# A DCN-v2 cross network on one core: filler matmuls as column tiles instead of full-array matmuls

## The chip, the cores and the metric

The kernel runs on one core of a Trainium2 chip. The metric is device time in microseconds (us), the median of several executions. The core has TensorE (PE) for matmuls, VectorE (DVE), ScalarE (ACT) and GpSimd (POOL) for the rest, and SyncE (SP), which here only issues DMAs. PEld in the profile is TensorE's weight load, which can run beside its matmuls.

## The reference

The input `x0` has 4096 rows of 416 features in bf16. There are six layers, each with a 416x416 matrix `ws[l]` and a bias `bs[l]`. The recurrence is

```
x = x0
for l in range(6):
    x = x0 * (x @ ws[l] + bs[l]) + x
return x
```

## The kernel before, in words

The kernel holds the activations transposed: features on the 128 partitions, rows of the batch along the free axis. The 416 features are three chunks of 128 and a tail of 32. The batch is cut into four slabs of 1024 rows, and each slab runs through six layers: 24 layer steps in all. A step takes the two halves (512 rows) of its slab through the 3x3 chunk products and adds the products with the tail. VectorE adds the bias and multiplies by `x0` on the way out of PSUM (line 445). ScalarE and GpSimd treat the tail (lines 474, 497 and 188). The `+ x` of the recurrence stays in PSUM: the matmuls of all layers of a slab accumulate there, and only the first one of a slab sets `start`.

Every engine has its own instruction list, written out by hand, and semaphores between them. Nothing is scheduled by a planner.

TensorE's array is addressed in tiles. The helper `tile_mm` (line 201 issues the matmul) uses 128 rows and 32 columns of the array, the q-th of four column tiles, and writes to the 32 PSUM partitions of that tile. The main matmuls are such groups of four: same moving operand, four different slices of 32 weight columns. The tail's products (lines 341 and 356) use 32 rows and 128 columns.

TensorE's list begins as follows.

1. `fill(14)` (line 233): 14 matmuls with constant operands of 1.0 (line 210). Their result in PSUM bank 7 is never read. They wait for no semaphore of the kernel.
2. A wait for the identity matrix, made by GpSimd, and for two loads of the input, each 256 rows, issued by SP and ACT as their first instructions (lines 113 and 460).
3. Twelve transposes of 128x128 (line 239), full-array, into PSUM. VectorE (line 420) and ScalarE (line 467) copy them to `x0T_sb`.
4. The first layer step of the first slab: for the first feature chunk three groups of column tiles, likewise for the second, then `third_input` (the transposes of 256 more rows, as column tiles), `tail_inputs`, `bias_sums`, and the third chunk. The weights of the first layer come in two loads, issued by SP (line 114) and ACT (line 461).

After this the steps follow each other on TensorE. At the end of the last slab the output is transposed back on TensorE, partly as column tiles (`out_chunk`), partly as full-array transposes (line 394), and stored.

The line numbers in the profile of before are those of this kernel.

## Time and profile before

| What | Value |
|---|---|
| Median of 5 runs | 131.71 us (131.37 to 131.87) |
| The profiled execution's own time | 131.87 us |
| Its span in the profile | 130.0 us |
| Time of that execution outside the span | 1.87 us |
| TensorE busy | 124.2 us (96%), 2406 matmuls |
| VectorE, ScalarE, GpSimd busy | 100.3, 71.4, 22.7 us |
| Mean granted TensorE clock | 0.992 |

The span runs from the first to the last instruction of the program on the core. A row of the profile names the line, the engine, the operation, the output and the inputs; `x14` is a count, and a mean or a minimum, median and maximum of durations in ns follow. "128*128 128x256" means an array tile of 128 rows by 128 columns, and an operand of 128 partitions with 256 elements. The ends of matmuls are modelled by the profiler, and matmuls overlap in the pipeline: how fast the array works is read from the distance between the starts, not from the duration of one. In the slices of the page each digit is a fortieth of the span.

### The profile page before, as it was taken

The page shows a single profiled execution, that of the slowest core. Times are in us where ns is not written, and L with a number is a line of the kernel's source. Part 1 is how long each engine was busy: PE and PEld are TensorE (multiplying, and loading weights), DVE is VectorE, ACT ScalarE, POOL GpSimd, SP SyncE. Part 2 cuts the span into 40 slices and gives each one's busy share as a digit, 9 for nine tenths or more (in the row PEclk, how much of TensorE's full clock was granted, in tenths as well). Part 3 has the DMA queues.
Part 4 walks back from the last instruction along what each step waited for, and adds up shares of the span by engine and source line. Part 5 has one row for each costly group of instructions (what it writes and reads, how often), then busy time and mean ns, then how long its engine had stood idle before and what let it go on. Part 6 is the DMA issues. An engine that isn't in the chain of part 4 may idle for free.

```text
span 130.0 us, 5323 instructions
## 1 busy us (share of the span) xinstructions
PE 124.2 (96%) x2406; PEld 62.4 (48%) x2406; DVE 100.3 (77%) x154; ACT 71.4 (55%) x164; POOL 22.7 (17%) x41
## 2 busy tenths in 40 slices
PE   7999999999999999999999999999999999999950
PEld 5654444444444444444444544444444444444530
DVE  2359779779779779779779779779779779779760
ACT  0537357377737357377737357377737357357650
POOL 7602202202202202202202212202202202202400
PEclk9999999999999999999999999999999999999996
DMA  4999989991009561000009434000009661000036
GB/s 127 284 281 298 215 117 228 155 194 40 8 12 145 113 212 55 5 0 5 0 17 172 83 120 147 0 5 0 5 14 131 122 225 42 5 0 5 3 84 183
DMA packets 32934, 12.54 MB, mean 96 GB/s; under 512 B 25338, under 2 KB 32912, under 8 KB 32912
## 3 DMA queue, kind: packets, MB, share of 16 engines
q1 hardware_dynamic: 31536, 11.49, 42.5%
q10 hardware_dynamic: 1184, 0.67, 1.8%
q8 instruction: 19, 0.31, 1.0%
q0 software_dynamic: 192, 0.05, 0.2%
q14 instruction: 3, 0.02, 0.1%
HBM read 2.90 MB, written 3.41 MB: 48 GB/s over the span
## 4 chain that ended last, share of the span: by engine, by line
PE 95%; DVE 1%; issue 0%; DVEq 0%
PE ps L201 81%; PE ps L341 10%; PE ps L210 2%; PE ps L239 1%; DVE o_sb L450 1%; PE ps L394 0%; DVE x0T_sb L425 0%; DVEq L33 0%; PE ps L356 0%
## 5 line engine op out<-in xcount | busy, mean ns | idle before, releaser
L445 DVE SCALAR_TENSOR_TENSOR xT_sb<-ps,cb_sb,x0T_sb 128x512 bf16<-128x512 f32 x120 | 80.8, 743 | 17.0 <-PE ps L341 17.0
L201 PE MATMUL ps<-xT_sb,w_sb 128*32 128x512 bf16 (+1 forms) x1680 | 89.0, 364 | 0.0
L201 PEld LDWEIGHTS ps<-xT_sb,w_sb 128*32 128x32 bf16 x1680 | 43.0, 97 | 38.7 <-issue 4.2
L474 ACT ACTIVATE xt_sb<-xt_sb 32x256 bf16<-32x256 bf16 x80 | 33.1, 414 | 16.6 <-POOL xt_sb L188 15.9
L497 ACT ACTIVATE t_sb<-ps,cb_sb 64x256 f32<-64x256 f32 x48 | 22.5, 468 | 30.7 <-PE ps L201 30.4
L188 POOL TENSOR_TENSOR xt_sb<-t_sb,x0t_sb 128x256 bf16<-128x256 f32 x20 | 13.4, 671 | 83.1 <-ACT t_sb L497 83.1
L201 PE MATMUL ps<-x0T_sb,w_sb 128*32 128x512 bf16 (+1 forms) x336 | 18.5, 365 | 0.0
L445 DVE SCALAR_TENSOR_TENSOR xo_sb<-ps,cb_sb,x0T_sb 128x512 bf16<-128x512 f32 x23 | 15.6, 744 | 3.4 <-PE ps L341 3.3
L341 PE MATMUL ps<-xt_sb,wt_sb 32*128 32x512 bf16 x80 | 12.3, 380 | 0.0
L201 PEld LDWEIGHTS ps<-x0T_sb,w_sb 128*32 128x32 bf16 x336 | 8.4, 97 | 7.6 <-issue 1.0
L510 ACT ACTIVATE x0t_sb<-x_sb 32x256 bf16<-32x256 bf16 x24 | 9.9, 413 | 0.4
L356 PE MATMUL ps<-xt_sb,wt_sb 32*128 32x512 bf16 x40 | 7.8, 385 | 0.0
L341 PE MATMUL ps<-xt_sb,wc_sb 32*128 32x256 bf16 x80 | 7.7, 268 | 0.0
L341 PEld LDWEIGHTS ps<-xt_sb,wt_sb 32*128 32x128 bf16 x80 | 2.4, 92 | 8.5 <-DVE xT_sb L445 8.5
L341 PEld LDWEIGHTS ps<-xt_sb,wc_sb 32*128 32x128 bf16 x80 | 3.9, 93 | 2.4 <-issue 0.2
L188 POOL TENSOR_TENSOR xot_sb<-t_sb,x0t_sb 128x256 bf16<-128x256 f32 x4 | 2.7, 672 | 12.6 <-ACT t_sb L497 12.6
L210 PE MATMUL ps<-const-bfloat16-1.0 128*128 128x256 bf16 x14 | 3.1, 415 | 0.8 <-PEq L547 0.8
L467 ACT ACT_TABLE_LOAD x1 | 1.3, 1283 | 3.4 <-issue 3.4
L420 DVE COPY x0T_sb<-ps 128x256 bf16<-128x256 bf16 x4 | 1.0, 290 | 2.7 <-PE ps L239 2.7
L210 PEld LDWEIGHTS ps<-const-bfloat16-1.0 128*128 128x128 bf16 x14 | 1.9, 141 | 1.6 <-issue 0.8
L341 PE MATMUL ps<-x0t_sb,wt_sb 32*128 32x512 bf16 x16 | 2.4, 380 | 0.0
L173 POOL DMA_DIRECT2D wc_sb<-in_ws_dram x4 | 2.2, 554 | 0.0
(45 smaller groups left out, 29.0 us busy)
## 6 DMA issues: line engine op xcount, KB each, us to landing
out_dram<-o_sb SPq DMA_DIRECT2D x3, 832.0 KB, 4.2
w_sb<-in_ws_dram SPq DMA_DIRECT2D x5, 312.0 KB, 4.1
xin_sb<-in_x_dram SPq DMA_DIRECT2D x2, 208.0 KB, 3.3
out_dram<-o_sb SPq DMA_DIRECT2D x1, 256.0 KB, 3.7
xin_sb<-in_x_dram ACTq DMA_DIRECT2D x1, 208.0 KB, 3.0
w_sb<-in_ws_dram ACTq DMA_DIRECT2D x1, 208.0 KB, 3.7
out_dram<-o_sb ACTq DMA_DIRECT2D x1, 208.0 KB, 3.2
out_dram<-o_sb SPq DMA_DIRECT2D x1, 208.0 KB, 3.2
```

The costliest lines, as they stand in the source:

```text
L173: pool.dma_start(wc_sb[lane(g), a:b, 32 * g:32 * g + 32], ws[a:b, DF:D, DF:D].rearrange("l p n -> p l n")).then_inc(s_wc[i], 16)
L188: pool.tensor_tensor(out=dst, in0=t32_sb[:, n % 2, :], in1=x0t_sb[:, s, 0:G], op=ALU.mult).then_inc(s_xt, 1)
L201: return pe.matmul(dst, lhsT=lhsT, rhs=rhs, start=start, stop=True, skip_group_check=True, tile_position=(0, 32 * q),)
L210: pe.matmul(ps[:, 7, 0:256], lhsT=const[:, 0:128], rhs=const, start=True, stop=True)
L239: ins = pe.transpose(out=psT[:, IN_BANKS[h][c], (j % 2) * 128:(j % 2 + 1) * 128], in_=xin_sb[:, j, c * 128:(c + 1) * 128], identity=ident[ ...
L341: return pe.matmul(dst, lhsT=lhsT, rhs=srct[lane(g), cols], start=l == 0 and start, stop=True, skip_group_check=True, tile_position=(32 * ...
L356: pe.matmul(ps[:, NC * h + 2, :], lhsT=wt_sb[lane(g), l, 0:128], rhs=srct[lane(g), :].rearrange("p (b r) -> p b r", b=2)[:, ::-1, :], star ...
L445: dve.scalar_tensor_tensor(out=dst, in0=ps[:, NC * half + c, :], scalar=cb_sb[:, c, l:l + 1], in1=x0T_sb[:, c, o:o + H], op0=ALU.add, op1= ...
L450: dve.tensor_copy(out=o_sb[:, j0 + 4:j0 + 8, 0:256], in_=psT[:, 4, :].rearrange("p (j d) -> p j d", d=256)).then_inc(s_oeD, 1)
L474: ins = act.activation(out=buf[lane(g), G:2 * G], in_=buf[lane(g ^ 1), 0:G], func=ACTF.Copy)
L497: ins = act.activation(out=t32_sb[HALVES[h], n % 2, :], in_=tail(h), func=ACTF.Identity, bias=cb_sb[HALVES[h], NC, l:l + 1],)
L510: ins = act.activation(out=x0t_sb[lane(g), s + 1, swap * G:(swap + 1) * G], in_=x4_sb[96:128, s, r * G:(r + 1) * G], func=ACTF.Copy,)
```

## The change

The filler's inner matmul is split. One matmul with a weight operand of 128x128 and a moving operand of 128x256 becomes four with 128x32 weights, one in each column tile, each with the same moving operand. The four write the same 128 partitions by 256 columns of bank 7 as the one did. The count of filler steps, 14, stays, as does their place in the list. The operands are the same constants.

```
             def fill(n):
                 for i in range(n):
-                    pe.matmul(ps[:, 7, 0:256], lhsT=const[:, 0:128], rhs=const, start=True, stop=True)
+                    for q in range(4):
+                        tile_mm(ps[lane(q), 7, 0:256], const[:, 0:32], const, q, True)
```

The helper it calls is the one of the main matmuls:

```
            def tile_mm(dst, lhsT, rhs, q, start):
                return pe.matmul(
                    dst, lhsT=lhsT, rhs=rhs, start=start, stop=True,
                    skip_group_check=True, tile_position=(0, 32 * q),
                )
```

TensorE's list then has 56 filler matmuls and 56 weight loads in place of 14 and 14. All lines after the filler move down by one, so that line 239 of before is line 240 after. The matmuls of the filler appear under line 201, the helper's, after the change.

## The prediction

> **What bounds the kernel now.** I read the page first: busy shares, the row of the granted clock, the chain that ended last. Then the start, where the change lies: the chain from 0 to 9 us, TensorE in order of time, and the durations by line.

> ```profile
> PE 124.2 (96%) x2406; PEld 62.4 (48%) x2406; DVE 100.3 (77%) x154; ACT 71.4 (55%) x164; POOL 22.7 (17%) x41
> ...
> PEclk9999999999999999999999999999999999999996
> ...
> PE 95%; DVE 1%; issue 0%; DVEq 0%
> PE ps L201 81%; PE ps L341 10%; PE ps L210 2%; PE ps L239 1%; DVE o_sb L450 1%; PE ps L394 0%; DVE x0T_sb L425 0%; DVEq L33 0%; PE ps L356 0%
> ```

> TensorE is busy for 96% of the span and makes up 95% of the chain. What delays its start is not made up later: the 24 layer steps run back to back on it. So the question is how the first 5 us change.

> ```profile
> 0.80 0.04 issue
> 0.85 3.14 PE ps L210 x14
> 3.99 1.27 PE ps L239 x12
> 5.26 1.55 PE ps L201 x32
> 6.81 0.03 issue
> 6.83 0.43 DVE x0T_sb L425
> ```

> The chain starts with the filler (L210) and goes on through the input transposes (L239) and the first layer (L201). The filler is thus on the path. Next, durations of one instruction (minimum, median, maximum):

> ```profile
> L210 PEld LDWEIGHTS ps<-const-bfloat16-1.0 x14: 105/147/147, 0.8 to 3.4; 128*128 128x128 bf16 x14
> L210 PE MATMUL ps<-const-bfloat16-1.0 x14: 371/418/418, 0.8 to 3.6; 128*128 128x256 bf16 x14
> ...
> L239 PE MATMUL ps<-ident,xin_sb x12: 298/311/312, 3.8 to 5.0; 128*128 128x128 bf16 x12
> ...
> L394 PE MATMUL ps<-ident,xo_sb x12: 219/219/229, 124.2 to 125.0; 128*128 128x128 bf16 x12
> ```

> The same transpose takes 311 ns at 3.8 to 5.0 us and 219 ns at the end. The row of the granted clock shows 9 in the first slices too, but these durations say that the array ran slower there. The spacing says by how much: twelve transposes start from 3.79 to 5.26 - 0.298 = 4.96, so (4.96 - 3.79) / 11 = 0.106 us apart. A transpose of four column tiles in the first layer is 0.056 us after the one before (28 instructions, seven groups of four, in 0.56 us, less 0.22 for the last). The filler: (0.85 + 3.14 - 0.418 - 0.85) / 13 = 0.21 us apart. So the array runs at half speed up to about 5.1 us, and at full speed from the first layer on:

> ```profile
> 0.85 3.14 PE L210 MATMUL ps<-const-bfloat16-1.0 128*128 128x256 bf16 x14 [0.85 <-PEq L547]
> 3.79 1.47 PE L239 MATMUL ps<-ident,xin_sb 128*128 128x128 bf16 x12
> 5.19 1.48 PE L201 MATMUL ps<-x0T_sb,w_sb 128*32 128x512 bf16 x24
> 6.49 0.56 PE L201 MATMUL ps<-ident,xin_sb 128*32 128x128 bf16 x27
> ```

> 24 matmuls of 512 columns are six groups of four; six groups in 1.48 us, with 0.38 for the last, are 0.22 us apart. At half speed they would be 0.43 apart. The full clock comes about 4.3 us after the first filler matmul (0.85 to 5.1).

> ```profile
> xin_sb<-in_x_dram SPq DMA_DIRECT2D x1, 208.0 KB, 2.8
> xin_sb<-in_x_dram ACTq DMA_DIRECT2D x1, 208.0 KB, 3.0
> ```

> Both input loads are issued at 0.81 and land at 3.6 and 3.8. The last filler matmul starts at 3.57 and streams until 3.57 + 0.21 = 3.79, when the first transpose starts. Filler and data end together here, with 0.2 us between them at most.

> **The change part by part.**

> Removed: 14 matmuls of 128x256 with 128-column weights, 0.21 us apart. Added: 56 matmuls of 32x256, in 14 groups of four column tiles. If the four run side by side, a group takes the time of one full matmul. The trace shows this at full speed: a group of 128 columns every 0.056 us, and the full-array L394 of 128 columns also every 0.056 ((124.64 - 124.24) / 7). No row shows column tiles at half speed. Bounds for a group: 0.21 us (all side by side) and 4 x 0.21 = 0.85 (one after the other). I take 0.21, because every group of four in this trace runs side by side; the term is 0.

> Weight loads: 14 of 147 ns become 56 of about 97 ns (the 128x32 rows of L201). In the first layer four such loads fit even in a group's 0.056 us, so in 0.21 us they are hidden. What hides them is the streaming of the group before; with that cover gone they would cost up to 56 x 0.097 = 5.4 us. [...]

> The filler's order, its waits (none) and its PSUM bank (7) stay. The transposes still wait for the same loads. No other engine's instructions, no DMA and no queue is moved. TensorE gets 84 more instructions, of 64 bytes (0.31 MB of instruction traffic over 4812 of them): 5 KB more to fetch. No fetch stall shows before; I cost it at 0, up to 0.1.

> The one new step: the array changes from column tiles to full tiles ahead of the first transpose. Before, filler and transposes had the same shape. Such a change shows a gap in the trace, from the end of streaming to the next start:

> ```profile
> 124.02 0.28 PE L201 MATMUL ps<-ident,xot_sb 128*32 128x128 bf16 x8
> 124.23 0.23 PE L394 MATMUL ps<-ident,xo_sb 128*128 128x128 bf16 x1
> ```

> The last column group starts at 124.02 + 0.28 - 0.22 = 124.08, streams 0.056, and the full-array transpose follows at 124.23: 0.09 to 0.10 us. The opposite change at 5.1 (the last transpose ends streaming at 4.96 + 0.107 = 5.07, the first layer starts at 5.19) took 0.12 us about when the clock came up. At half speed: 0.10 as lower bound, and 0.12 plus a full weight load in the open (0.105, the shortest L210 and so about one L239 load) = 0.23 as upper bound. I take 0.14, nearer to the 0.12 row, which lies in the same place.

> So the first transpose starts at about 3.93. If the clock still comes at 5.1, eleven transposes run at 0.107 until then, and the last at 0.056: end at 5.16 in place of 5.07. The next change of shape costs 0.10 rather than 0.12, and the first layer starts at 5.26 to 5.28 instead of 5.19: +0.08. By the bounds: 0.05 and 0.13; with no help from the clock 0.23. I take +0.1. Late next is the first layer with all behind it: the weights for it (issued at 1.3, landing in 3.0 and 3.7 us) are there by 5.1, so no load hides the shift. VectorE's copies (L425) and the bias sums wait on TensorE and move with it.

> The sum against the profiled execution: span 130.0 + 0.1, and 131.87 + 0.1 = 131.97. That execution is the slowest of the five; the median is 131.71, so the forecast is 131.8. The runs themselves range over 0.5 us, and about 0.3% (0.4 us) is what a measurement of this kernel can tell from no change; +0.1 is within it.

> **The rivals.**

> Later full clock (slower). The gate may count a column tile as less work than a full-array matmul. Then the clock would come only after the transposes have done what filler and transposes do now. Speaking for it: nothing in the trace shows column tiles raising the clock; they start just after it came. Against: from 5.19 on nearly all work is column tiles, and the granted clock stays at 1.00 until 128 us. Price: full speed 4.27 us after the first transpose, at 3.93 + 4.27 = 8.2. Transposes until 5.21, change of shape 0.12, six groups of 512 at 0.43 until 7.9, three groups of 128 at 0.107 until 8.2, the other seven at 0.056 until 8.6. That work now ends at 7.05: +1.55, or 133.3. It decides (over 0.4) from about 0.6 us of delay, since each microsecond of half speed costs half a microsecond.

> [...]

> Earlier full clock (faster). If the gate counts instructions or streams of data, four tiles weigh more than one full matmul. For: each group streams the moving operand four times. Against: no row. The filler would then end early, but the transposes still wait for the load at 3.6: start at 3.69, 12 x 0.056 = 0.67, change of shape 0.10, first layer at 4.46 instead of 5.19: -0.73. Its weights (1.34 + 3.7 = 5.04 for the second block, wanted at 5.1) just suffice. That gives 131.0, and no earlier clock gives more. It decides from about one microsecond earlier, at 4.1.

> The tiles do not run side by side at half speed (slower). Group 0.85 us: five groups until 5.1, the other nine at 0.43 until 9.0 instead of 3.79; transposes then save 0.6. About +4.6, or 136. Against it: every group of four in the trace overlaps.

> **How the numbers follow.** Same mechanism with +0.1: 0.42. Later clock: 0.31. Earlier clock: 0.20. Not side by side: 0.04. The remaining 0.03 are runs that scatter over the bound to either side, with a little more to the slower. That the clock keeps its time is the likeliest single case, but no row supports it for a filler of column tiles, hence the weight of the two clock cases. Faster 0.21, same 0.42, slower 0.37. The range reaches from the earlier clock, 131.0, to the later one with the estimate by windows rounded up, 133.5. The likeliest case's own range is 131.4 to 132.1: the shift from 0.05 to 0.23 and the runs' scatter.

> **What the changed kernel's profile would show.** If right: 56 matmuls of 128x256 with 32 columns of weights, in 14 groups about 0.21 us apart, from 0.85 to 3.8; first transposes at 3.9 to 4.0, of 311 ns; the last one or two shorter; the first layer at about 5.3 with 379 ns matmuls 0.22 us apart. A later clock would show first-layer groups 0.43 us apart. An earlier one would show filler groups 0.11 us apart and TensorE idle until the input lands. Tiles one after the other would show in a filler beyond 4 us. What would make it wrong above all is the moment at which the full clock comes.

## The result and the profile after

The changed kernel takes 130.64 us (median of 44 runs, 130.21 to 132.03), the kernel before 131.41 us (86 runs, 130.53 to 134.06). The ratio is 0.9949, with an interval of 0.9936 to 0.9963: faster by 0.5%. The forecast was 131.8 with a range from 131.0, so both the sign and the range were missed.

The page of the changed kernel (profiled execution 130.63 us, span 128.8):

```profile
PE 124.0 (96%) x2448; PEld 62.3 (48%) x2448; DVE 100.3 (78%) x154; ACT 71.3 (55%) x164; POOL 22.8 (18%) x41
...
PE 91%; DMA 4%; ACTq 1%; DVE 1%; DVEq 0%; issue 0%
PE ps L201 81%; PE ps L342 10%; DMA xtl_sb<-in_x_dram 4%; DVE o_sb L451 1%; PE ps L395 0%; ACTq L462 0%; ACTq L461 0%; DVEq L33 0%; PE ps L357 0%
```

TensorE is as busy as before, and at the start the chain now goes through an input load (`xtl_sb`, the tail's features) instead of the filler. TensorE in order of time, and the durations of the transposes:

```profile
0.85 3.18 PE L201 MATMUL ps<-const-bfloat16-1.0 128*32 128x256 bf16 x56 [0.85 <-PEq L548]
3.96 0.91 PE L240 MATMUL ps<-ident,xin_sb 128*128 128x128 bf16 x12
4.98 1.48 PE L201 MATMUL ps<-x0T_sb,w_sb 128*32 128x512 bf16 x24
6.44 0.82 PE L201 MATMUL ps<-ident,xin_sb 128*32 128x128 bf16 x27
```

```profile
L240 PE MATMUL ps<-ident,xin_sb x12: 219/219/288, 4.0 to 4.6; 128*128 128x128 bf16 x12
```

The filler has the predicted length, the transposes start at 3.96, with 3.93 predicted. In this execution the full clock comes at about 4.1 us, a microsecond earlier than in the profiled execution of before: most transposes take 219 ns, not 311. That looks like the rival "earlier full clock". It is not where the time went. The next groups wait for the third input load (6.44) and for the tail's (landed at 6.97), and the row tiles of the first layer step (the tail's products, on 32 rows of the array) start at 8.31 us, against 8.36 before: 0.04 us of the gain in the span, which is 130.04 - 128.81 = 1.23 us.

The rest lies in two places. The first is in the second layer step. Weight loads of the row tiles before, and the same stretch after:

```profile
13.24 0.09 PEld L341 LDWEIGHTS ps<-xt_sb,wt_sb 32*128 32x128 bf16 x1
13.56 0.09 PEld L341 LDWEIGHTS ps<-xt_sb,wc_sb 32*128 32x128 bf16 x1 [0.23 <-issue]
```

```profile
13.20 0.09 PEld L342 LDWEIGHTS ps<-xt_sb,wt_sb 32*128 32x128 bf16 x1
13.20 0.10 PEld L342 LDWEIGHTS ps<-xt_sb,wc_sb 32*128 32x128 bf16 x1
```

Before, TensorE has nothing to load for 0.23 us in the middle of a group, and the profile names no engine or DMA as the releaser ("issue"). This costs 0.12 us on the path: the third step starts 0.16 us earlier after the change, the second only 0.04.

The second place is the end. TensorE reaches its last transposes 0.16 us earlier (L394 at 124.23 before, L395 at 124.08 after); the other 1.07 us come after that. The stores of the output on SyncE, before and after, with start and length of the issue:

```profile
123.99 0.37 SPq L147 DMA_DIRECT2D out_dram<-o_sb  x1
125.19 1.15 SPq L150 DMA_DIRECT2D out_dram<-o_sb  x1
126.44 0.46 SPq L153 DMA_DIRECT2D out_dram<-o_sb  x1
```

```profile
123.83 0.37 SPq L147 DMA_DIRECT2D out_dram<-o_sb  x1
125.03 0.37 SPq L150 DMA_DIRECT2D out_dram<-o_sb  x1
125.50 0.46 SPq L153 DMA_DIRECT2D out_dram<-o_sb  x1
```

Before, the second store is issued for 1.15 us instead of 0.37, and the third waits behind it. The times from issue to landing (last column), before and after:

```profile
out_dram<-o_sb SPq DMA_DIRECT2D x1, 256.0 KB, 3.7
out_dram<-o_sb ACTq DMA_DIRECT2D x1, 208.0 KB, 3.2
out_dram<-o_sb SPq DMA_DIRECT2D x1, 208.0 KB, 3.2
out_dram<-o_sb SPq DMA_DIRECT2D x1, 160.0 KB, 3.3
```

```profile
out_dram<-o_sb SPq DMA_DIRECT2D x1, 256.0 KB, 2.3
out_dram<-o_sb SPq DMA_DIRECT2D x1, 208.0 KB, 2.3
out_dram<-o_sb ACTq DMA_DIRECT2D x1, 208.0 KB, 2.7
out_dram<-o_sb SPq DMA_DIRECT2D x1, 160.0 KB, 2.1
```

What stands between them is seen in the DMA traffic from 118.5 to 125.5 us, GB/s in 40 slices of 0.175 us, and in the line of the instruction queue in that window; before first, then after:

```profile
GB/s 0 0 0 0 0 0 0 0 0 0 0 0 0 0 0 0 0 0 0 0 0 47 0 0 0 0 0 0 0 0 0 0 0 0 94 0 73 298 310 287
...
q8 instruction: 1, 0.02, 1.3%
```

```profile
GB/s 0 0 0 0 0 0 0 0 0 0 0 0 0 0 0 0 0 0 0 0 47 0 0 0 0 0 94 0 0 0 0 0 0 0 0 50 313 313 319 316
...
q8 instruction: 1, 0.02, 0.9%
```

The slice with 94 GB/s is one transfer of 94 x 0.175 = 16 KB: a load of instructions. (The slice with 47 is a load of 8 KB on another queue.) Before, it falls into slice 34 (124.45 to 124.62; 124.52 in the trace's record, 1.4 us long), half a microsecond after the first store was issued. After, it falls into slice 26 (123.05 to 123.22), before the first store. The kernel before has 19 such loads of 16 KB, 0.31 MB: over the 4860 instructions of TensorE's list in the trace that is 64 bytes each, and so 256 instructions to a load, an estimate from these numbers.

So a new theory stood against that of the clock. **Fetch theory**: the gain is not what the 56 matmuls do on the array, but that their 84 extra instructions shift all later ones in TensorE's list. Its instructions come in the 16 KB blocks of these loads, and the points in the work at which a block is called for would move with the list. **Number theory** (many small matmuls bring the full clock earlier) and other theories of the filler were the rivals.

### The profile page after: what moved, and what is told of

The parts are those of the page before. It is cut to its first block, busy times and chain, and to the rows that moved or that the text cites. A ratio compares the mean times of both kernels' runs of the same rounds, so it can differ in the third digit from the quotient of the medians.

```text
span 128.8 us, 5407 instructions
## 1 busy us (share of the span) xinstructions
PE 124.0 (96%) x2448; PEld 62.3 (48%) x2448; DVE 100.3 (78%) x154; ACT 71.3 (55%) x164; POOL 22.8 (18%) x41
## 4 chain that ended last, share of the span: by engine, by line
PE 91%; DMA 4%; ACTq 1%; DVE 1%; DVEq 0%; issue 0%
PE ps L201 81%; PE ps L342 10%; DMA xtl_sb<-in_x_dram 4%; DVE o_sb L451 1%; PE ps L395 0%; ACTq L462 0%; ACTq L461 0%; DVEq L33 0%; PE ps L357 0%
## 5 line engine op out<-in xcount | busy, mean ns | idle before, releaser
L201 PE MATMUL ps<-xT_sb,w_sb 128*32 128x512 bf16 (+1 forms) x1680 | 89.0, 364 | 0.0
L201 PEld LDWEIGHTS ps<-xT_sb,w_sb 128*32 128x32 bf16 x1680 | 43.1, 97 | 38.8 <-issue 4.2
L201 PE MATMUL ps<-x0T_sb,w_sb 128*32 128x512 bf16 (+1 forms) x336 | 18.5, 365 | 0.1
L201 PEld LDWEIGHTS ps<-x0T_sb,w_sb 128*32 128x32 bf16 x336 | 8.5, 97 | 7.6 <-issue 1.1
L201 PE MATMUL ps<-const-bfloat16-1.0 128*32 128x256 bf16 x56 | 3.2, 418 | 0.8 <-PEq L548 0.8
L201 PEld LDWEIGHTS ps<-const-bfloat16-1.0 128*32 128x32 bf16 x56 | 2.3, 143 | 1.2 <-issue 0.8
## 6 DMA issues: line engine op xcount, KB each, us to landing
xin_sb<-in_x_dram SPq DMA_DIRECT2D x2, 208.0 KB, 3.7
xin_sb<-in_x_dram ACTq DMA_DIRECT2D x1, 208.0 KB, 3.2
w_sb<-in_ws_dram ACTq DMA_DIRECT2D x1, 208.0 KB, 3.5
out_dram<-o_sb SPq DMA_DIRECT2D x1, 208.0 KB, 2.3
out_dram<-o_sb ACTq DMA_DIRECT2D x1, 208.0 KB, 2.7
```

The costliest lines, as they stand in the source:

```text
L201: return pe.matmul(dst, lhsT=lhsT, rhs=rhs, start=start, stop=True, skip_group_check=True, tile_position=(0, 32 * q),)
```

## The experiments

All kernels were compared with the kernel before on the same chip, mostly with 12 timed runs. The medians of before were 131.6 to 131.8 us in these comparisons. Each diff is against the kernel before, unless it says otherwise.

**The form of the filler.** The first four kernels were made when the clock was still the suspect.

```
-                    pe.matmul(ps[:, 7, 0:256], lhsT=const[:, 0:128], rhs=const, start=True, stop=True)
+                    tile_mm(ps[lane(0), 7, 0:256], const[:, 0:32], const, 0, True)
```

> Filler: each step is one column tile of 32 columns alone (14 small matmuls), the same length in time, a quarter of the array. Three theories of why four column tiles bring the full clock earlier. Time theory: the gate counts the time in which TensorE is busy with anything; then one tile is as good as one full-array matmul, about 131.4 us like the kernel before. Columns theory: it counts the share of the array in use; then one tile counts a quarter, the full clock comes later than before and the time is 132 us or more. Number theory (matmuls, tiles or weight loads are counted, whatever their size): one tile per step is as good as one full matmul per step, 131.4 us. If the gain is not in the clock at all but in the change of shape ahead of the transposes, this filler has that change too and gains as much as four tiles: 130.7 us.

131.99 us, ratio 1.0032 (1.0004 to 1.0061).

```
-                    pe.matmul(ps[:, 7, 0:256], lhsT=const[:, 0:128], rhs=const, start=True, stop=True)
+                    for g in range(4):
+                        pe.matmul(
+                            ps[:, (1, 2, 6, 7)[g], 0:256], lhsT=const[lane(g), 0:128], rhs=const[lane(g), :],
+                            start=True, stop=True, skip_group_check=True, tile_position=(32 * g, 0),
+                        )
```

> Filler: each step is four row tiles of 32 rows by 128 columns, side by side, into four PSUM banks. The moving data that enter the array are those of one full-array matmul, 128 rows in all, while four column tiles read four times as many. Number theory: four matmuls per step as with column tiles, about 130.7 us. Data theory (the gate weighs the rows that stream in): as before, about 131.4 us. Columns theory: all of the array is in use, as before, about 131.4 us.

130.85 us, ratio 0.9928 (0.9904 to 0.9951).

```
-                for i in range(n):
-                    pe.matmul(ps[:, 7, 0:256], lhsT=const[:, 0:128], rhs=const, start=True, stop=True)
+                for i in range(2 * n):
+                    pe.matmul(ps[:, 7, 0:128], lhsT=const[:, 0:128], rhs=const[:, 0:128], start=True, stop=True)
```

> Filler: 28 full-array matmuls of 128 columns instead of 14 of 256, the same length in time, twice as many matmuls and weight loads. Number theory: halfway or more towards four tiles, 130.7 to 131.1 us. Time and data theories: as before, about 131.4 us.

130.98 us, ratio 0.9940 (0.9913 to 0.9968).

```
-            fill(14)
+            fill(0)
```

> No filler at all. It prices what the full clock is worth here: without work before 3.7 us the clock comes 2 to 3 us later than before, at half a microsecond per microsecond, less what the loads hide: 132.2 to 133 us. If the filler's only effect were its place on the path, the time would fall or stay, 131.4 us or less.

132.93 us, ratio 1.0095 (1.0057 to 1.0132).

Taken alone these four fit the number theory perfectly: four row tiles and 28 short matmuls gain what four column tiles gain, one tile per step gains nothing, no filler loses. But they fit a count of instructions equally, and two things spoke for that. First, the end of the span lay 3.96 us after the start of TensorE's last matmul in the kernel with row tiles, as in the changed kernel, 4.11 with short matmuls, 4.55 with one tile, and 5.03 before. A clock that comes early can't shorten the end: it was full in both until 128.0 us before and 127.0 after, 3.0 and 2.2 us past the start of that matmul. Second, the moment of the full clock is spread much alike in both kernels. Its fall at the end is in the record of the granted clock:

```profile
127.90:128.00 0.10, 0.00 (x0) 0.00 (x0) 0.00 (x0) 0.00 (x0) 0.00 (x0) 0.97 1.06 269
128.00:128.10 0.10, 0.00 (x0) 0.00 (x0) 0.00 (x0) 0.00 (x0) 0.00 (x0) 0.50 1.13 326
```

```profile
126.90:127.00 0.10, 0.00 (x0) 0.00 (x0) 0.00 (x0) 0.00 (x0) 0.00 (x0) 1.00 1.00 333
127.00:127.10 0.10, 0.00 (x0) 0.00 (x0) 0.00 (x0) 0.00 (x0) 0.00 (x0) 0.56 1.08 358
```

The third column from the right is the granted clock: half from 128.0 us before and from 127.0 after, each 122.9 us after the full clock came (5.1 and 4.1). With this distance, the mean granted clock and the span of an execution give an estimate of the moment: span x (2 x clock - 1) - 122.9. Executions in which the clock does not fall within the span are left out (12 and 11). The estimate takes the distance for granted: it was the same in 15 of the 18 traces of this case, longer in two (one block more, pad at 7.4 us) and shorter without filler. For 112 executions of the kernel before (all comparisons together) the estimates run from 3.6 to 7.0 us, for 58 of the changed kernel from 3.6 to 6.5; the medians are 5.4 and 4.9. At like moments the times differ by much the same: with the clock at 3.5 to 4.4 us the medians are 131.32 before and 130.41 after, with 4.4 to 5.2 us 131.53 and 130.65, with 6 to 7 us 132.09 and 131.20. So the moment costs up to 0.8 us within either kernel, and the gain of about 0.9 us does not come from it; the half microsecond between the medians is worth some 0.15 us, estimated from the same numbers.

**The place in the list.** The next four kernels set the fetch theory against the number theory.

```
-                for i in range(n):
-                    pe.matmul(ps[:, 7, 0:256], lhsT=const[:, 0:128], rhs=const, start=True, stop=True)
+                for i in range(n // 2):
+                    pe.matmul(ps[:, 7, :], lhsT=const[:, 0:128], rhs=const2, start=True, stop=True)
```

(`const2` is the same constant, 512 wide.)

> Filler: 7 full-array matmuls of 512 columns instead of 14 of 256. Same length in time, no change of shape, 14 instructions fewer on TensorE's list. Fetch theory: the gain has nothing to do with what the array does, but with where the last 16 KB load of TensorE's instructions falls. Before, it falls at 124.5 us among the output stores; 84 more instructions ahead of it let it come earlier, at 123.1. With 14 instructions fewer it comes 0.35 us later or, as with no filler at all, is not called for any more; in the second case the time falls by about 1 us to 130.5 to 130.8, in the first it stays at 131.4 to 131.9. Number theory (many small matmuls bring the full clock earlier): half as many matmuls as before, slower, 131.8 us or more.

131.64 us, ratio 1.0013 (0.9978 to 1.0047). The first of the two cases of the fetch theory: the load still came, at 124.91 in its profiled execution, 0.61 us after the first store's issue. Half as many matmuls as before cost nothing, against the number theory.

```
+                for i in range(2 * n + 7):
+                    for q in range(4):
+                        tile_mm(ps[lane(q), 7, 0:100], const[:, 0:32], const[:, 0:100], q, True)
+                for q in range(2):
+                    tile_mm(ps[lane(q), 7, 0:84], const[:, 0:32], const[:, 0:84], q, True)
```

> Filler: 142 column-tile matmuls, 35 groups of four with 100 columns and two more with 84, of the same length in time together. That is 256 instructions more on TensorE's list than before, one 16 KB block exactly, so that the last instruction load is called for at the same point of the work as before. Fetch theory: the gain is lost again, about 131.5 to 131.9 us, with the last instruction load 0.5 us ahead of TensorE's last matmul and the second output store's issue of 0.6 to 1.2 us. Number theory: at least as fast as four tiles, 130.6 us.

133.12 us, ratio 1.0106 (1.0056 to 1.0157), from 6 runs. The gain is gone and more: the fetch theory has the side right, but its size missed by more than a microsecond. The end is slow, as expected (4.84 us after the last matmul), though the second store's issue takes 0.37 us and not the 0.6 to 1.2 expected. The excess has two parts in the profiled execution. The row tiles of the first step start at 9.13 us, against 8.36 before, because the third and the tail's input loads land late; the kernel's first instruction load comes at 5.11, among them, but that it held them up was not tested. And there is a stall in the second layer step, at the same instruction as in the kernel before, which makes this step 0.82 us longer than the others, against 0.12 before:

```profile
14.03 0.09 PEld L344 LDWEIGHTS ps<-xt_sb,wt_sb 32*128 32x128 bf16 x1
15.06 0.09 PEld L344 LDWEIGHTS ps<-xt_sb,wc_sb 32*128 32x128 bf16 x1 [0.93 <-issue]
```

Here 0.93 us of idle time where the kernel before has 0.23, between the same two weight loads, with the list shifted by one block exactly. The kernel with one tile per step, whose list is not shifted at all, has 0.76 at the same place. This ties the place of the stall to the list, though not its length (see below).

```
+            for i in range(42):
+                tile_mm(ps[lane(i % 4), 7, 384:392], const[:, 0:32], const[:, 0:8], i % 4, True)
```

> The filler as before; 42 tiny matmuls (84 instructions, 8 columns each) at the very end of TensorE's list. The list is as long as with four column tiles, but nothing before the end moves. Fetch theory: no gain, 131.4 to 131.9 us, since the last load falls where it fell. If the length of the list as such counted (its alignment in memory or the number of blocks), 130.7 us.

131.39 us, ratio 0.9986 (0.9951 to 1.0021): no gain from a longer list. The load falls among the stores (0.40 us after the first one's issue), and the end is slow, 4.43 us after the start of the last output transpose.

```
                 pe.wait_ge(s_inD, 5)
+                for i in range(42):
+                    tile_mm(ps[lane(i % 4), 6, 384:392], const[:, 0:32], const[:, 0:8], i % 4, True)
```

> The filler as before; the 42 tiny matmuls (84 instructions) ahead of the bias sums at 7.4 us, on the path. They cost 0.2 to 0.4 us there (sixteen tiny matmuls of the bias sums start within 0.1 us before). Fetch theory: the last load comes 1.4 us earlier as with four tiles, 1.0 us is gained at the end, net 0.6 to 0.8 us faster than before. Number theory and any theory of the filler: slower than before by 0.2 to 0.4 us.

132.00 us, ratio 1.0040 (1.0004 to 1.0075). A miss for the fetch theory as it was put: slower by 0.4, where 0.6 to 0.8 us of gain were expected. Its end is the fast one (3.96 us after the last matmul). But the 84 instructions at this place brought new stalls early on, the first of them here:

```profile
10.75 0.82 PE L201 MATMUL ps<-x0T_sb,w_sb 128*32 128x512 bf16 x12
12.17 2.13 PE L201 MATMUL ps<-xT_sb,w_sb 128*32 128x512 bf16 x36 [0.60 <-issue]
```

TensorE idles from 11.57 to 12.17 with no releaser shown, while the second layer's weights (landed at 8.6) and VectorE's first result (10.1) were there. In the kernel before there is no such gap between these two groups. A second stall follows at 18.57. The steps with the two stalls take 0.78 and 0.89 us longer than the 4.87 us of the others, and the first step starts 0.21 later: that, less the 0.12 of the stall before and 1.07 at the end, is the 0.70 us by which this span is longer. So the gain at the end was there, and a shift of the list must be tried where it does not disturb the start.

**The same shift without touching the start.** Waits on semaphores that were reached long ago, in layer steps that keep TensorE busy throughout (70.0 of 70.0 us from 25 to 95 us in the profile of before):

```
                     for m in range(NC):
+                        if n >= 4 and pad[0] > 0:
+                            pad[0] -= 1
+                            pe.wait_ge(s_set, 2)
+                            pe.wait_ge(s_zero, 2)
+                            ...
                         chunk(m, 1).then_inc(s_mb, 1)
```

> The filler as before. 84 instructions more on TensorE's list, as many as with four column tiles, but as waits on semaphores that were reached long ago, two at a time in the layer steps 5 to 18, where TensorE's queue is full and they cost the array nothing. The start is untouched. Fetch theory: the last load of instructions comes about 1.4 us earlier in the work than before, before the first output store, and 0.7 to 1.0 us are gained, as with four tiles, though the filler is the old one. Any theory of the filler or of the clock gate: no change against before, within 0.2 us.

130.82 us, ratio 0.9937 (0.9903 to 0.9971). The filler is the old one, and the gain is there. The DMA traffic from 118.5 us on and the stores:

```profile
GB/s 0 0 0 0 0 0 0 0 0 0 0 0 0 0 0 0 0 0 0 0 0 47 0 0 0 0 94 0 0 0 0 0 0 0 0 0 181 322 316 313
```

```profile
123.93 0.37 SPq L147 DMA_DIRECT2D out_dram<-o_sb  x1
125.12 0.37 SPq L150 DMA_DIRECT2D out_dram<-o_sb  x1
125.59 0.47 SPq L153 DMA_DIRECT2D out_dram<-o_sb  x1
```

The load is in slice 26 as with column tiles, and no issue is held up. (The waits begin at layer step 5, counted from 1. Two of these lines make one instruction: four lines in each of 42 chunks add 84 to TensorE's list, 4944 instead of 4860.)

In the next kernel there are fewer of these waits (the first two of the lines in 28 chunks, which add 28 instructions, and the old filler):

```
                     for m in range(NC):
+                        if n >= 4 and pad[0] > 0:
+                            pad[0] -= 1
+                            pe.wait_ge(s_set, 2)
+                            pe.wait_ge(s_zero, 2)
                         chunk(m, 1).then_inc(s_mb, 1)
```

> As the last one with 28 such waits only, the shift of the filler of 28 short matmuls. Fetch theory: the last load comes 0.7 us earlier in the work, just about at the issue of the first store, and 0.5 to 0.9 us are gained. Theories of the filler: no change.

131.36 us, ratio 0.9963 (0.9925 to 1.0001): about half of the gain, less clear than expected. In the profiled execution the load came 0.18 us before the first store's issue, and the end was fast (4.09); but the twelve runs spread from 130.44 to 132.24.

The next one starts from the changed kernel and shifts on to a full block (the diff is against the changed kernel; six lines in each of 58 chunks add 174 instructions):

```
                     for m in range(NC):
+                        if n >= 4 and pad[0] > 0:
+                            pad[0] -= 1
+                            pe.wait_ge(s_set, 2)
+                            ...
+                            pe.wait_ge(s_te0, 1)
                         chunk(m, 1).then_inc(s_mb, 1)
```

> The filler of four column tiles, and 174 such waits in the layer steps from 4 on, so that TensorE's list is 258 instructions longer than before, within two of a block of 256, and the start is that of the changed kernel. Fetch theory: the last load falls at the output stores again, the gain is lost, 131.3 to 131.9 us. Theories of the filler or the clock gate: the gain stays, 130.6 to 130.9 us.

131.09 us, ratio 0.9954 (0.9922 to 0.9986). Lost in part only. The load came 0.02 us after the first store's issue in the profiled execution. The stores on SyncE, start and length of the issue:

```profile
124.09 0.37 SPq L147 DMA_DIRECT2D out_dram<-o_sb  x1
125.28 0.53 SPq L150 DMA_DIRECT2D out_dram<-o_sb  x1
125.91 0.45 SPq L153 DMA_DIRECT2D out_dram<-o_sb  x1
```

Their times from issue to landing (last column):

```profile
out_dram<-o_sb SPq DMA_DIRECT2D x1, 256.0 KB, 3.2
out_dram<-o_sb SPq DMA_DIRECT2D x1, 208.0 KB, 2.7
out_dram<-o_sb ACTq DMA_DIRECT2D x1, 208.0 KB, 3.2
out_dram<-o_sb SPq DMA_DIRECT2D x1, 160.0 KB, 2.6
```

The stores are slow again (3.2 against 2.3 for the first), though less than before.

The changed kernel itself beside these three:

> The changed kernel once more, on the same chip as the three others, so that its gain and theirs are compared without the spread between chips: 0.5% faster than before. The kernel with 84 waits should be as fast or 0.1 us faster, since it has no change of shape ahead of the transposes.

130.68 us, ratio 0.9926 (0.9891 to 0.9961). The changed kernel and the one with 84 waits are alike within their intervals.

**What is left.** Three more kernels and the changed kernel for comparison. The first has the same waits as the one with column tiles above, in 50 chunks instead of 58, 150 instructions (`pad = [50]` for `pad = [58]`).

> As the kernel of four column tiles with 174 waits, with 150 of them. There the last load of instructions came 0.5 us earlier against the end than in the kernel before, and only part of the gain was lost. 24 instructions fewer move it 0.6 us later, to where it was before. Fetch theory: 131.3 to 131.8 us, the gain of the changed kernel gone but for the 0.1 to 0.4 us that the stall in the second layer step costs the kernel before. Theories of the filler: the gain stays.

131.11 us, ratio 0.9947 (0.9917 to 0.9977): the gain was not lost. In the profiled execution no instruction load came between 121.5 us and the end of the span (the next one started at 130.0, after it), and the first store landed in 2.3 us: the 24 instructions moved the call past the end of the work, not to where it was before. The runs spread from 130.40 to 131.69; whether the load came among the stores in the slower of them can't be seen, since only one execution has a trace.

The diff of the next, against the changed kernel, is `fill(13)` for `fill(14)`:

> Four column tiles, 13 filler steps instead of 14. The filler ends 0.21 us earlier, so that the change of shape lies beside the wait for the input, which lands at 3.6 to 3.7 us. List: 8 instructions shorter. If the change of shape is a cost of this version, 0.1 us faster than the changed kernel; if the loads that follow (the third input, the tail) set the pace anyway, the same.

131.00 us, ratio 0.9950 (0.9921 to 0.9980).

```
-                    ins = pe.transpose(
-                        out=psT[:, IN_BANKS[h][c], (j % 2) * 128:(j % 2 + 1) * 128],
-                        in_=xin_sb[:, j, c * 128:(c + 1) * 128], identity=ident[:, :],
-                    )
+                    for q in range(4):
+                        f0 = c * 128 + 32 * q
+                        ins = tile_mm(
+                            ps[lane(q), IN_BANKS[h][c], (j % 2) * 128:(j % 2 + 1) * 128],
+                            xin_sb[:, j, f0:f0 + 32], ident[:, :], q, True,
+                        )
```

> As the last, and the twelve input transposes as column tiles too (48 matmuls against the identity, copied from fp32), so that there is no change of shape between filler, transposes and first layer. Two gaps of 0.10 to 0.17 us go, VectorE's and ScalarE's copies of the first 512 rows take 0.1 us longer each. 0.0 to 0.2 us faster than the changed kernel. The list is 148 instructions longer than before, and the last load comes well ahead of the stores.

132.11 us, ratio 1.0025 (0.9989 to 1.0062): slower than the changed kernel by over a microsecond, against 0.0 to 0.2 us of gain expected. The end is fast (3.96 us after the last matmul). In the profiled execution TensorE's last matmul starts 2.02 us later than in that of the changed kernel: 0.66 us are lost before the row tiles of the first step (8.98 against 8.31, with the full clock at 6.3 us), and 1.36 in three stalls with no releaser shown, in the first, second and third step.

> The changed kernel on the same chip, to compare the three others with: about 0.6% faster than before.

130.85 us, ratio 0.9948 (0.9921 to 0.9975). A filler step less changes nothing against it. No kernel tried beats the changed one clearly.

**The stalls without a releaser.** The traces show what they are. From 8.5 us to the end of the work TensorE starts an instruction at least every 0.34 us in all 18 traces, save for seven stalls, and all seven end at one of three places of its list, counted in the order of starts: instruction 450, 706 or 962, a block of 256 apart.

| Kernel | Instruction | Its start (us) | Landing of its load, us before that |
|---|---|---|---|
| one tile | 450 | 14.23 | 1.36 |
| one block more | 706 | 15.06 | 1.45 |
| pad at 7.4 us | 450 | 12.17 | 1.27 |
| pad at 7.4 us | 706 | 19.66 | 1.43 |
| transposes as column tiles too | 450 | 10.40 | 1.42 |
| transposes as column tiles too | 706 | 17.25 | 1.51 |
| transposes as column tiles too | 962 | 24.63 | 1.67 |

The load meant is the first in the trace for 450, the second for 706, and so on. In no trace does an instruction at such a place (450 and every 256th after it, 327 in all) start sooner than 1.2 us after its load landed; the weight load at 13.56 us in the kernel before is instruction 450 and starts 1.24 us after. So these are waits for instructions. How long they are depends on when the load starts, and that is not fixed by the list: with the same list up to there, it starts at 11.36 us in the kernel before, 11.92 with one tile and 11.23 with 28 waits, which all stall, and at 10.05 with the pad at the very end and 9.48 with 84 waits, which do not. The 0.12 us in the second step can thus not be put down to the shift for certain.

The kernels in one view, from the profiled executions: instructions added ahead of the end of TensorE's list, start of the last instruction load within the span against the issue of the first store (from the trace's records), landing of the first store, and the end of the span counted from the start of TensorE's last matmul, without the padding behind it (us).

| Kernel | Added | Load - store | Landing | End |
|---|---|---|---|---|
| no filler | -28 | -2.74 | 2.3 | 3.96 |
| 150 waits, column tiles | 234 | -2.74 | 2.3 | 3.95 |
| 7 long matmuls | -14 | +0.61 | 3.1 | 4.63 |
| before | 0 | +0.53 | 3.7 | 5.03 |
| one tile | 0 | +0.42 | 3.3 | 4.55 |
| padded at the very end | 0 | +0.40 | 3.1 | 4.43 |
| one block more | 256 | +0.79 | 3.1 | 4.84 |
| 174 waits, column tiles | 258 | +0.02 | 3.2 | 4.42 |
| 28 waits | 28 | -0.18 | 2.8 | 4.09 |
| short matmuls | 28 | -0.17 | 2.8 | 4.11 |
| changed kernel | 84 | -0.77 | 2.3 | 3.96 |
| changed kernel, two more | 84 | -1.10, -0.98 | 2.3 | 3.98, 3.97 |
| 13 filler steps, column tiles | 76 | -1.01 | 2.3 | 3.98 |
| transposes as column tiles too | 148 | -2.32 | 2.3 | 3.96 |
| 84 waits, old filler | 84 | -0.77 | 2.3 | 3.96 |
| row tiles | 84 | -0.83 | 2.3 | 3.96 |
| pad at 7.4 us | 84 | -0.80 | 2.3 | 3.96 |

Whatever the filler is made of, the first store lands in 2.3 us where the load starts 0.77 us or more ahead of it, in 2.8 where it starts 0.2 us ahead, and in 3.1 to 3.7 where it falls among the stores. A block more (256, or 258 with the 174 waits) brings the slow end back, so by these two rows the place counts modulo a block. All rows follow this, though the slow ends differ (4.42 to 5.03) and only the kernel before has an issue as long as 1.15 us.

## Why the prediction was wrong

**The step that failed** is in the paragraph of "The change part by part" on what stays: "TensorE gets 84 more instructions, of 64 bytes (0.31 MB of instruction traffic over 4812 of them): 5 KB more to fetch. No fetch stall shows before; I cost it at 0, up to 0.1." The price of the bytes is right, the load count stayed at 19. What counts is where in the work the blocks are called for: with 84 instructions more, 1.07 us were gone from the end in the profiled executions, and by the runs 0.96 us with 84 waits (131.78 - 130.82), 1.10 with the changed kernel beside them and 0.77 in the first comparison. The sign of this term was not considered at all: it was bounded below by 0 without a reason that excludes a gain. (0.30 us of the distance between 131.8 and 130.64 is not this step but the base: five runs had given 131.71 for the kernel before, 86 gave 131.41.)

And the sentence "No fetch stall shows before" was wrong. The trace of before has the 0.23 us of idle time at 13.56 us with no releaser, and a store whose issue takes 1.15 us where its neighbours take 0.37 and 0.46. Both were to be seen by asking for the second step and for the last 6 us; the prediction read the first 9 us and the share of TensorE in the chain. That chain ends at 125.8 us with VectorE; the last 4 us of the span, where the stores land, are in none of its lines.

**The start** went as forecast up to the transposes. Four tiles run side by side at half speed (the filler takes 3.18 us with 56, 3.14 with 14), the loads of weights are hidden (2.3 us of busy time within these 3.18), and the first transpose starts at 3.96, with 3.93 predicted. The loads took 143 ns each in the mean, not the predicted 97, but the 14 of before took 141: the narrower loads show no cost here. The predicted cost of the change of shape, +0.1 us on the path, is smaller than that if it exists: where the full clock comes at 5.44 us in both, the row tiles of the first step start at 8.54 with column tiles and at 8.49 with short full-array matmuls, 0.05 us apart; a shorter filler brought nothing. In nearly all other profiled executions the input also lands later than in that of before (ScalarE's load after 3.1 to 3.4 us, against 3.0), which can cover it.

**The rivals.** "Earlier full clock" was given 131.0 us and a chance of 0.20, and the profile after looks like it. The moments are spread much alike in both kernels, and the 84 waits give the gain with the old filler: as the source of the gain its mechanism is refuted, and its sign was right by accident. "Later full clock" did not occur, nor tiles one after the other. The upper end of the range, 133.5, takes in an estimate by windows of the clock, a term that no run shows. What the runs show is a moment of the full clock that varies: 4.1, 4.6 and 5.4 us in three profiled executions of the changed kernel, and 3.6 to 7.0 by the estimates for the kernel before, which leave out every execution with a later fall; it was worth up to 0.8 us. The profile of one execution shows one draw of this, so two profiles should not be compared for it.

**What stays open.** How a load of instructions holds up a store is not shown. The traces of before and after show that a 16 KB transfer lasts 0.9 to 1.6 us (1.4 and 1.0 for the last one), and the traces of all kernels that the landing of the stores around it, and the issue of the second one, are longer by a part of that up to all of it. When exactly a block is called for stays open too: the last load of the changed kernel came 0.77 to 1.10 us ahead of the first store in three executions. Both tables follow blocks of 256 instructions, a 16 KB load each. Only seven of the 327 places above have a gap of over 0.34 us between starts, but there a load costs up to 1.1 us, and at the end of this kernel about 1 us of 131.

## What to carry to other kernels

Count the instructions that an edit adds to or takes from an engine's list: on a list of some 4900 instructions a shift of 84 moved an instruction load of 16 KB off the output stores and was worth 0.8 to 1.1 us, more than anything that the instructions did. Read the end of the span as closely as the place of the edit, above all an issue or a landing that is longer than its like, and look for "issue" as the only releaser. When a variant gains, test whether idle instructions in a neutral place gain the same, before its purpose is believed.
